# Constants as transposed rows, and roots and exponentials side by side, in a matmul-bound kernel

## The chip, the cores and the metric

One core of a Trainium2 chip. The metric is device time in microseconds (us) of one execution, taken over several runs. Engines are called as the profile calls them: PE is TensorE, DVE is VectorE, ACT is ScalarE, POOL is GpSimd, SP is SyncE. "L501" is a line of the kernel's source, so the same statement has another number in another version.

## The reference, cut to what matters

```
xn  = layernorm(x)                               # x: 2048 x 576, bf16
h_t = Lam_bar * h_{t-1} + B_bar xn_t             # 576 complex states, Lam_bar = exp(dt * Lambda), dt = exp(log_dt)
A   = 2 Re(C h) + xn * Dskip
B   = (sigmoid(xn Wg) * (xn Wu)) Wd              # 576 -> 4608 -> 576
out = x + A + B
```

Almost all the work is in B. The recurrence needs, per state, `exp` of `log_dt`, a decay, and tables of sines and cosines of angle times position. The constants are three vectors of 576 numbers: `log_dt`, `Lambda_re`, `Lambda_im`.

## The kernel before

The sequence is cut into four blocks of 512 rows. PE computes "groups": 18 matmuls of 64 x 128 by 64 x 512 that fill one pair of PSUM banks with gate and up values. ACT reads the pair (a sigmoid into `sT`, a copy into `uT`), and DVE multiplies them to `hT`. After 24 groups come eight down steps of 24 matmuls (later ones carry the matmuls of C as well; the last step has 42). Four PSUM pairs rotate (code cut and condensed here and below):

```
PE_SLOTS = 4
def ps_pair(name):
    return psum.tile([P, 2, TB], FP32, name=name, tag="ps")     # PE_SLOTS bufs
...
def evac(self):                                  # of a gate/up group
    nc.scalar.activation(sT[:], self.ps[:, 0, :], ACT.Sigmoid)
    nc.scalar.copy(uT[:], self.ps[:, 1, :])
    nc.vector.tensor_mul(h[:], sT[:], uT[:])
    bg.step(T_GROUP - 0.42 - 0.2)                # let DVE's background work go on
```

DVE's other work stands in a background queue that gets a credit of 1.33 us per group. At the start, block 0's LN goes through PE transposes. Then two groups start, and block 1's LN and the constants follow through the queue:

```
for g in start_groups: g.mms(slice(2 * P, TB))           # second halves of g0 and g1
for tt in range(4, 8): bg.add(1.05, lambda tt=tt: ln_stats(tt))
bg.gap()
bg.add(0.0, lambda: ln_std(1, 0, TT_B))                  # the square roots, on ACT
bg.add(0.2, lambda: ln_recip(1, 0, TT_B))
...                                                      # norms and DMA transposes of block 1
for tt in range(0, 8): bg.add(1.25, lambda tt=tt: ln_resid(tt))
bg.gap()
bg.add(1.0, exp_first, ready=lambda: consts_at[0] is not None and consts_at[0] + 4 <= bg.now)
bg.gap()
bg.add(1.5, angles_small)
...                                                      # ten angle tables of 1.35
bg.step(3.2)
for g in start_groups:
    g.evac(); used(g); bg.step(4.5)
```

The constants were fetched by nine loads on POOL's queue that scatter single numbers over partitions, 35 us into the profiled run (the end of the function is cut):

```
def load_consts():
    for (dst, src) in ((ldt, A_log_dt), (lre, A_Lambda_re), (lim, A_Lambda_im)):
        nc.gpsimd.dma_start(dst[:, 0:PT], src[0:R0].rearrange("(a p) -> p a", p=P))
        for h0 in (0, H):
            nc.gpsimd.dma_start(dst[h0:h0 + H, PT:NU], src[R0:NS].rearrange("(a b) -> a b", b=1))
```

## Time and profile before

| | before |
|---|---|
| time at the outset, median of 3 | 509.22 us (508.66 to 509.3) |
| the profiled run | 508.32 us, span 506.5 |
| PE, DVE, ACT, POOL busy | 99%, 64%, 40%, 19% |
| first real group starts | 8.48 |
| last matmul ends | 502.76 |

A timeline line has start, duration, engine, source line, operation, tiles and count; a bracket names idle time before it and what ended it. The waits view has total us, number of times and the longest. A view of one source line, used for the end of the program, has count, then duration in ns (least, median, most), then the first and the last start. The profiled run took 508.32 us and the timed runs 509.2.

### The profile page before, as it was taken

Reading aid. Unit: us, or ns where it says so; the run is one execution under the profiler, and the core shown is the slowest. Engines: PE = TensorE matmul, PEld = TensorE weight load, DVE = VectorE, ACT = ScalarE, POOL = GpSimd, SP = SyncE. Lnnn points to the kernel's source line nnn. Section 1 sums busy time; section 2 is a strip of 40 time slices with the busy share of each in tenths; the row PEclk is TensorE's granted clock in tenths of the full one; section 3 lists DMA queues with packets and bytes.
Section 4 is the critical chain, followed back from the end, with each engine's and each line's share of the span. In section 5 each row is a group of like instructions: output and inputs, shape, how many; then the busy total and the mean of one; then the engine's idle time right before and its main releaser. Section 6 shows DMA issues by size and latency. Waiting matters only on the chain.

```text
span 506.5 us, 10662 instructions
## 1 busy us (share of the span) xinstructions
PE 500.9 (99%) x4536; PEld 290.1 (57%) x4536; DVE 324.1 (64%) x703; ACT 204.9 (40%) x368; POOL 96.9 (19%) x143
## 2 busy tenths in 40 slices
PE   8999999999999999999999999999999999999997
PEld 6444575444477444477754444774444774446775
DVE  6964999886888797868878767786765222221111
ACT  4767623556500756520035655006555005553000
POOL 7138420123100043110001231000431001300000
PEclk9999999999999999999999999999999999999999
DMA  8999895246220099261430652200753201600001
GB/s 211 206 181 163 204 188 98 55 110 141 49 48 25 1 145 199 58 149 37 89 77 11 155 132 55 49 25 1 160 114 79 48 25 39 171 1 4 33 25 36
DMA packets 42959, 45.59 MB, mean 90 GB/s; under 512 B 30496, under 2 KB 34336, under 8 KB 42912
## 3 DMA queue, kind: packets, MB, share of 16 engines
q0 software_dynamic: 12672, 34.23, 31.1%
q1 hardware_dynamic: 29808, 10.33, 10.7%
q8 instruction: 35, 0.57, 0.5%
q10 hardware_dynamic: 432, 0.37, 0.2%
q14 instruction: 12, 0.10, 0.1%
HBM read 34.36 MB, written 2.36 MB: 72 GB/s over the span
## 4 chain that ended last, share of the span: by engine, by line
PE 94%; DVE 3%; ACT 1%; DMA 1%; issue 0%
PE pgu L495 52%; PE pd L569 34%; PE pbu L524 7%; DVE sctab L325 1%; DVE rnd L324 1%; DMA xt<-in_A_x_dram 1%; DVE ang L349 1%; PE ptr L741 0%; DVE hT L504 0%; ACT xT L744 0%; DVE bnst L224 0%; ACT L328 0%; ACT uT L502 0%; ACT L501 0%; ACT sT L501 0%
## 5 line engine op out<-in xcount | busy, mean ns | idle before, releaser
L495 PE MATMUL pgu<-xT,wgu 64*128 64x512 bf16 (+1 forms) x2628 | 283.7, 373 | 0.0
L495 PEld LDWEIGHTS <-wgu 64*128 64x128 bf16 x2628 | 127.6, 94 | 151.1 <-issue 0.5
L569 PE MATMUL pd<-wd,hT 128*128 128x288 bf16 x1152 | 144.8, 286 | 0.4 <-DVE hT L504 0.4
L501 ACT ACTIVATE sT<-pgu 128x512 bf16<-128x512 f32 x144 | 86.4, 600 | 120.4 <-PE pgu L495 110.3
L569 PEld LDWEIGHTS <-hT 128*128 128x128 bf16 x1152 | 112.1, 98 | 31.3 <-DVE hT L504 1.5
L504 DVE TENSOR_TENSOR hT<-sT,uT 128x512 bf16<-128x512 bf16 x144 | 60.7, 423 | 100.3 <-ACT uT L502 100.1
L502 ACT CAST uT<-pgu 128x512 bf16<-128x512 f32 x144 | 83.9, 583 | 0.0
L154 POOL DMA_DIRECT2D wgu<-in_B_w_gate_dram x36 | 27.9, 776 | 227.2 <-PE pgu L495 208.2
L160 POOL DMA_DIRECT2D wd<-in_B_w_down_dram x36 | 26.6, 755 | 100.2 <-PE pd L569 100.2
L530 ACT COPY bure<-pbu 128x512 f32<-128x512 f32 x16 | 9.4, 588 | 87.8 <-PE pbu L524 75.4
L589 DVE TENSOR_TENSOR acc<-acc,pd 128x576 f32<-128x576 f32 x32 | 24.1, 752 | 24.5 <-PE pd L569 24.5
L586 DVE TENSOR_TENSOR ob<-acc,pd 128x576 bf16<-128x576 f32 x15 | 11.3, 754 | 38.0 <-PE pd L569 38.0
L524 PE MATMUL pbu<-xT,bt 64*128 64x512 bf16 x288 | 33.7, 376 | 0.0
L569 PEld LDWEIGHTS <-hst 128*128 128x128 bf16 x288 | 28.2, 98 | 7.1
L154 POOL DMA_DIRECT2D wgu<-in_B_w_up_dram x36 | 26.8, 745 | 2.7 <-DMA wgu<-in_B_w_up_dram 1.9
L569 PE MATMUL pd<-ctre,hst 128*128 128x288 bf16 x128 | 26.5, 286 | 0.0
L569 PE MATMUL pd<-ctim,hst 128*128 128x288 bf16 x128 | 26.5, 286 | 0.0
L439 DVE TENSOR_TENSOR_SCAN gre<-r,g0re,wrim 128x512 bf16<-128x512 f32 x20 | 25.6, 1279 | 0.0
L524 PEld LDWEIGHTS <-bt 64*128 64x128 bf16 x288 | 13.7, 94 | 17.1 <-issue 0.7
L446 DVE TENSOR_TENSOR_SCAN gim<-r,g0im,wrim 128x512 bf16<-128x512 f32 x16 | 20.4, 1275 | 0.0
L224 DVE BATCH_NORM_STATS2 bnst<-xt 128x6 f32<-128x288 bf16 x32 | 12.6, 435 | 2.2 <-DMA xt<-in_A_x_dram 2.2
L501 ACT ACT_TABLE_LOAD x6 | 7.7, 1283 | 15.5 <-PE pgu L495 15.4
(113 smaller groups left out, 280.8 us busy)
## 6 DMA issues: line engine op xcount, KB each, us to landing
wgu<-in_B_w_gate_dram POOLq DMA_DIRECT2D x36, 288.0 KB, 4.4
wgu<-in_B_w_up_dram POOLq DMA_DIRECT2D x36, 288.0 KB, 5.2
wd<-in_B_w_down_dram POOLq DMA_DIRECT2D x36, 288.0 KB, 6.1
out_dram<-ob SPq DMA_DIRECT2D x15, 144.0 KB, 1.8
xt<-in_A_x_dram SPq DMA_DIRECT2D x10, 144.0 KB, 2.8
xt<-in_A_x_dram POOLq DMA_DIRECT2D x4, 144.0 KB, 6.6
bt<-ctre POOLq DMA_DIRECT2D x2, 288.0 KB, 7.2
bt<-ctim POOLq DMA_DIRECT2D x2, 288.0 KB, 8.0
```

Source lines behind the costliest of these rows:

```text
L154: eng.dma_start(w[rows, :, :], src[:, fs].rearrange("(c p) f -> p c f", p=H))
L160: nc.gpsimd.dma_start(wd[:], B_w_down[f0:f0 + FP * P, :].rearrange("(n p) d -> p n d", p=P))
L224: nc.vector.bn_stats(st[:, gi, :], xt[:, gi * DH:(gi + 1) * DH])
L439: nc.vector.tensor_tensor_scan(gre[:], r_bc, w[:, 0, :], g0re[:, col], ALU.mult, ALU.add)
L446: nc.vector.tensor_tensor_scan(gim[:], r_bc, w[:, 1, :], g0im[:, col], ALU.mult, ALU.add)
L495: nc.tensor.matmul(self.ps[:, gi, cols], w[rows, c, fs], xT[self.nb][rows, c, cols], start=c == 0, stop=c == NH - 1)
L501: nc.scalar.activation(sT[:], self.ps[:, 0, :], ACT.Sigmoid)
L502: nc.scalar.copy(uT[:], self.ps[:, 1, :])
L504: nc.vector.tensor_mul(h[:], sT[:], uT[:])
L524: nc.tensor.matmul(out, w, xT[self.nb][rows, c, ts_], start=c == 0, stop=c == NH - 1)
L569: nc.tensor.matmul(out, lhsT, rhs[:, a * DH:(a + 1) * DH], start=i == 0, stop=i == n - 1)
L589: nc.vector.tensor_add(halves(acc[:]), halves(acc[:]), pd[:, :, 0:DH])
```

## The change

The intent was to take the nine scattered loads off POOL's queue, to have the exponentials early so that the angle tables don't crowd the first down steps, to save one table load on ACT by putting roots and exponentials side by side, and to shorten the tail of the last step. The core of the diff, cut:

```
+    crows = consts.tile([3 * NH, H], BF16, name="crows")
+    for i, src in enumerate((A_log_dt, A_Lambda_re, A_Lambda_im)):
+        nc.sync.dma_start(crows[i * NH:(i + 1) * NH, :], src.rearrange("(a p) -> a p", p=H))
+    def consts_transpose(ps):
+        for half in (slice(0, H), slice(H, P)):
+            nc.tensor.transpose(ps[half, 0:3 * NH], crows[:], ident[0:3 * NH, 0:3 * NH])
+    def consts_copy(ps): ...                     # three copies on DVE, PSUM -> cvals
...
     def exp_first():
-        nc.scalar.activation(dt[:], ldt[:], ACT.Exp)
-        nc.vector.tensor_mul(r5[:], dt[:], lre[:])
-        nc.scalar.activation(r5[:], r5[:], ACT.Exp)
+        nc.scalar.activation(dt[:], ldt, ACT.Exp)
+        for a in range(NU):
+            nc.scalar.activation(r5[:, a:a + 1], lre[:, a:a + 1], ACT.Exp, scale=dt[:, a:a + 1])
...
-            for a, eng in ((0, nc.sync), (1, nc.scalar)):      # last step: 288 + 288 columns
+            for eng, cs in ((nc.sync, slice(0, D - P)), (nc.scalar, slice(D - P, D))):   # 448 + 128
...
-    for g in start_groups:
-        g.mms(slice(2 * P, TB))
-    ...                                          # the queue shown above
+    start_groups[0].mms(slice(2 * P, TB))
+    consts_transpose(ptrs[1][:, NH, :])
+    consts_copy(ptrs[1][:, NH, :])
+    start_groups[1].mms(slice(2 * P, TB))
+    for tt in range(TT_B, 2 * TT_B): ln_stats(tt)
+    for g in start_groups: g.evac(); used(g)
+    ln_std(1, 0, TT_B)
+    exp_first()
+    ln_recip(1, 0, TT_B)
+    ...                                          # norms and transposes in place, then the residuals and angles in the queue
```

More of the change, by code (lines that the diff above doesn't have):

```diff
@@ L166 @@
         load_x(tt, nc.sync if tt % 2 == 0 else nc.scalar)
-    for pr in range(2):
-        load_wgu((0, pr), nc.gpsimd, nc.gpsimd)
+    load_wgu((0, 0), nc.gpsimd, nc.gpsimd)
+    load_wgu((0, 1), nc.gpsimd, nc.gpsimd)
     for tt in range(TT_B, 2 * TT_B):
@@ L184, with consts_copy @@
     xn_bufs = [consts.tile([P, NH, 2, H], BF16, name=f"xn{i}") for i in range(XN_BUFS)]
-    lre = consts.tile([P, NU], FP32, name="lre")
-    lim = consts.tile([P, NU], FP32, name="lim")
-    ldt = consts.tile([P, NU], FP32, name="ldt")
-    consts_at = [None]
-    def load_consts():
-        for (dst, src) in ((ldt, A_log_dt), (lre, A_Lambda_re), (lim, A_Lambda_im)):
-            nc.gpsimd.dma_start(dst[:, 0:PT], src[0:R0].rearrange("(a p) -> p a", p=P))
-            for h0 in (0, H):
-                nc.gpsimd.dma_start(dst[h0:h0 + H, PT:NU], src[R0:NS].rearrange("(a b) -> a b", b=1))
-        consts_at[0] = bg.now
+    cvals = consts.tile([P, 3, NU], FP32, name="cvals")
+    ldt, lre, lim = (cvals[:, i, :] for i in range(3))
+    crows = consts.tile([3 * NH, H], BF16, name="crows")
[4 more added lines that the diff above has]
+            nc.tensor.transpose(ps[half, 0:3 * NH], crows[:], ident[0:3 * NH, 0:3 * NH])
+    def consts_copy(ps):
+        rows = ps[:, 0:3 * NH].rearrange("p (i a) -> p i a", a=NH)
+        nc.vector.tensor_copy(cvals[0:H, :, :], rows[0:H, :, 0:NH:2])
+        nc.vector.tensor_copy(cvals[H:P, :, 0:PT], rows[H:P, :, 1:NH:2])
+        nc.vector.tensor_copy(cvals[H:P, :, PT:NU], rows[H:P, :, NH - 1:NH])
     iota = ssmp.tile([P, TB], FP32, name="iota", tag="buim", bufs=2)
@@ L327, in exp_first @@
     def exp_first():
-        nc.scalar.activation(dt[:], ldt[:], ACT.Exp)
-        nc.vector.tensor_mul(r5[:], dt[:], lre[:])
-        nc.scalar.activation(r5[:], r5[:], ACT.Exp)
+        nc.scalar.activation(dt[:], ldt, ACT.Exp)
+        for a in range(NU):
+            nc.scalar.activation(r5[:, a:a + 1], lre[:, a:a + 1], ACT.Exp, scale=dt[:, a:a + 1])
     def angles_small():
-        nc.vector.tensor_mul(thc[:], dt[:], lim[:])
+        nc.vector.tensor_mul(thc[:], dt[:], lim)
         nc.vector.tensor_scalar_mul(thc[:], thc[:], 1.0 / TWO_PI)
@@ L365, in per_state_q @@
         nc.vector.tensor_mul(ni[:], r5[:], sn)
-        nc.vector.tensor_mul(m1[:], lre[:], lre[:])
-        nc.vector.tensor_mul(m2[:], lim[:], lim[:])
+        nc.vector.tensor_mul(m1[:], lre, lre)
+        nc.vector.tensor_mul(m2[:], lim, lim)
         nc.vector.tensor_add(m1[:], m1[:], m2[:])
         nc.vector.reciprocal(m1[:], m1[:])
-        nc.vector.tensor_mul(qre[:], nr[:], lre[:])
-        nc.vector.tensor_mul(m2[:], ni[:], lim[:])
+        nc.vector.tensor_mul(qre[:], nr[:], lre)
+        nc.vector.tensor_mul(m2[:], ni[:], lim)
         nc.vector.tensor_add(qre[:], qre[:], m2[:])
         nc.vector.tensor_mul(qre[:], qre[:], m1[:])
-        nc.vector.tensor_mul(qim[:], ni[:], lre[:])
-        nc.vector.tensor_mul(m2[:], nr[:], lim[:])
+        nc.vector.tensor_mul(qim[:], ni[:], lre)
+        nc.vector.tensor_mul(m2[:], nr[:], lim)
         nc.vector.tensor_sub(qim[:], qim[:], m2[:])
@@ L572, in d_step @@
             ob = lnp.tile([P, D], BF16, name="ob", bufs=2)
-            for a, eng in ((0, nc.sync), (1, nc.scalar)):
-                cs = slice(a * DH, (a + 1) * DH)
-                pd = ps_pair("pd")
+            for eng, cs in ((nc.sync, slice(0, D - P)), (nc.scalar, slice(D - P, D))):
+                pd = ps_pair("pd")[:, 0, 0:cs.stop - cs.start]
                 for i in range(n):
-                    mm(pd[:, 0, 0:DH], i, a)
-                nc.vector.tensor_add(ob[:, cs], acc[:, cs], pd[:, 0, 0:DH])
+                    lhsT, rhs = terms[i]
+                    nc.tensor.matmul(pd, lhsT, rhs[:, cs], start=i == 0, stop=i == n - 1)
+                nc.vector.tensor_add(ob[:, cs], acc[:, cs], pd)
                 eng.dma_start(o[tt * P:(tt + 1) * P, cs], ob[:, cs])
@@ L726 @@
     start_groups = [GateUp(0, f, 0) for f in range(2)]
-    ptrs = [psum.tile([P, NH, P], BF16, name="ptr", tag="ps") for _ in range(2)]
+    ptrs = [psum.tile([P, NH + 1, P], BF16, name="ptr", tag="ps") for _ in range(2)]
     for g in start_groups:
@@ L770 @@
         start_copy(tt, slice(5, NH), nc.vector.tensor_copy)
-    for g in start_groups:
-        g.mms(slice(2 * P, TB))
-    for tt in range(TT_B, 2 * TT_B):
-        bg.add(1.05, lambda tt=tt: ln_stats(tt))
-    bg.gap()
-    bg.add(0.0, lambda: ln_std(1, 0, TT_B))
-    bg.add(0.2, lambda: ln_recip(1, 0, TT_B))
-    for tt in range(TT_B, 2 * TT_B):
-        bg.add(0.9, lambda tt=tt: ln_norm(tt))
-        bg.add(0.0, lambda tt=tt: ln_dma_transpose(tt))
-    bg.add(0.0, lambda: ln_done.add(1))
-    bg.add(0.0, bg.owe)
+    start_groups[0].mms(slice(2 * P, TB))
+    consts_transpose(ptrs[1][:, NH, :])
+    consts_copy(ptrs[1][:, NH, :])
+    start_groups[1].mms(slice(2 * P, TB))
+    for tt in range(TT_B, 2 * TT_B):
+        ln_stats(tt)
+    for g in start_groups:
+        g.evac()
+        used(g)
+    ln_std(1, 0, TT_B)
+    exp_first()
+    ln_recip(1, 0, TT_B)
+    for tt in range(TT_B, 2 * TT_B):
+        ln_norm(tt)
+        ln_dma_transpose(tt)
+    ln_done.add(1)
+    bg.owe()
     for tt in range(0, 2 * TT_B):
         bg.add(1.25, lambda tt=tt: ln_resid(tt))
-    bg.gap()
-    bg.add(1.0, exp_first, ready=lambda: consts_at[0] is not None and consts_at[0] + 4 <= bg.now)
-    bg.gap()
     bg.add(1.5, angles_small)
@@ L791 @@
             bg.add(1.35, lambda pt=pt, which=which: angle(pt, which))
-    bg.step(3.2)
-    for g in start_groups:
-        g.evac()
-        used(g)
-        bg.step(4.5)
     def catch_up_ln(nb):
@@ L821 @@
                 run_groups([GateUp(slot, f, nb) for (f, nb) in order[:8]])
-                catch_up_ln(1)
                 order = order[8:]
-                side_loads.extend([load_consts] + bt_loads)
+                side_loads.extend(bt_loads)
             run_groups([GateUp(slot, f, nb) for (f, nb) in order])
```

## The prediction

> **What bounds the kernel now.** I read the page's busy times first, then who TensorE waited for, then the engines' timelines in the first 64 us and the last 12 us.
>
> ```profile
> PE 500.9 (99%) x4536; PEld 290.1 (57%) x4536; DVE 324.1 (64%) x703; ACT 204.9 (40%) x368; POOL 96.9 (19%) x143
> ...
> PE pgu L733 <- DVE warm L182: 1.3, 1, 1.3
> PE pd L569 <- DVE hT L504: 0.4, 1, 0.4
> PE ptr L741 <- DVE xn L249: 0.3, 1, 0.3
> ```
>
> TensorE is busy 500.9 of 506.5 us. Its recorded waits sum to 2.0 us, and only one of them lies in the body: 0.4 us before the first down-projection matmuls, behind an hT. Busy alone proves little for a pipelined engine, so I check the pitch: in the chain of waits a gate/up group (18 matmuls of 512 columns) takes 1.94 us, 108 ns each, and the last down step advances every 0.122 us per 288 columns. The work is thus 144 groups x 1.94 = 279.8, the state inputs 4 x (4 x 1.94 + 0.98) = 35.0, and the down and C matmuls 1440 x 0.1224 = 176.3: together 491.1 us. Between the first real group at 8.48 and the last matmul at 502.76 lie 494.3 us, 1.1 of which are input transposes. The body holds barely 2 us that a schedule could win. Any change of this kind is worth tenths, unless it makes TensorE stop.
>
> What it could win or lose is in the start, on ACT and DVE:
>
> ```profile
> 11.61 1.28 ACT L501 ACT_TABLE_LOAD   x1
> 12.90 0.60 ACT L501 ACTIVATE sT<-pgu 128x512 bf16<-128x512 f32 x1
> 13.39 0.58 ACT L502 CAST uT<-pgu 128x512 bf16<-128x512 f32 x1
> 13.99 1.28 ACT L228 ACT_TABLE_LOAD   x1
> 16.16 0.30 ACT L228 ACTIVATE rstd<-mv,eps_t 128x4 f32<-128x4 f32 x1 [0.89 <-DVE mv L225]
> 16.48 1.28 ACT L501 ACT_TABLE_LOAD   x1
> 17.77 0.60 ACT L501 ACTIVATE sT<-pgu 128x512 bf16<-128x512 f32 x1
> 18.26 0.58 ACT L502 CAST uT<-pgu 128x512 bf16<-128x512 f32 x1
> 18.73 0.61 ACT L501 ACTIVATE sT<-pgu 128x512 bf16<-128x512 f32 x1
> ```
>
> This is ACT's timeline. The first sigmoid group (I count groups g0, g1, ... in emission order) is evacuated at 12.90, then ACT loads the square-root table, waits 0.89 us for the last statistics, takes the roots, and loads the sigmoid table again. g1 is read only at 17.77. From a later undisturbed group (g11, read at 33.28, as it ends) and 1.943 us per group, g1 ended at 33.28 - 10 x 1.943 = 13.85. It was read 3.9 us late and TensorE did not feel it, because four PSUM pairs rotate.
>
> ```profile
> 42.14 1.28 ACT L328 ACT_TABLE_LOAD   x1
> 43.44 0.21 ACT L328 ACTIVATE dt<-ldt 128x5 f32<-128x5 f32 x1
> 43.88 0.21 ACT L330 ACTIVATE r<-r 128x5 f32<-128x5 f32 x1 [0.23 <-DVE r L329]
> 44.10 1.28 ACT L501 ACT_TABLE_LOAD   x1
> 45.40 0.60 ACT L501 ACTIVATE sT<-pgu 128x512 bf16<-128x512 f32 x1
> ...
> 59.23 0.42 DVE L504 TENSOR_TENSOR hT<-sT,uT 128x512 bf16<-128x512 bf16 x1
> ...
> 59.70 2.50 PE L569 MATMUL pd<-wd,hT 128*128 128x288 bf16 x19 [0.35 <-DVE hT L504]
> ```
>
> ACT, then DVE, then TensorE. The exponentials come 30 us later with two more table loads. The angle tables wait for them, so DVE starts the angles only at 48.2 with credit saved up. From there each hT stands behind one angle until 59.65, when the last hT of the first down step appears. TensorE lost 0.35 us to it.
>
> **What the Trainium skill says.** "ScalarE: Activation LUTs", section "What ACT_TABLE_LOAD costs", has about 1283 ns for the load plus about 1380 ns of drain per switch. The trace agrees on the load (1.28 us at all four places above) but shows no drain: a load starts 0.01 us after the copy's end (13.39 + 0.58, next at 13.99) and the activation follows it 0.01 us later. I count 1.28. Section "Table sets: the hidden batching unit" says to batch by set; roots and exponentials are in different sets there, so putting them side by side saves one return to sigmoid, not a load of its own. The trace's 12 loads should become 11. "Perfetto Trace Analysis", section "Matmuls", says that independent groups should rotate through PSUM banks so that evacuation overlaps matmuls; this kernel rotates four pairs, which is the limit that I use below. "TensorE: Matmul & The Clock Gate", section "Back-to-back issue gap", has about 81 ns per matmul of 128 columns with its weight load; here 20 warm-up matmuls of that size, each with its weight load, start from 7.14 to 8.2 us, 56 ns apart, and I use that.
>
> **The change part by part.**
> (a) Constants. Nine descriptor-poor loads on the POOL queue (35.0 to 40.5 us, 5.5 us of POOL) become three row loads on SP behind the first x tiles. TensorE never waited for a weight load in that stretch, so 0 on the path. In their place stand two tiny transposes between g0's and g1's second halves (0.1 us of TensorE) and three small copies on DVE. I put a copy at 0.2 us, from the 0.17 us of the other 5-column DVE operations plus a little for PSUM: 0.6 us.
> (b) LN of block 1 in place. The DVE copies of xT ended at 12.04, and the statistics began at once. Now DVE must wait for the transposes, which follow the end of g0, 13.85 - 0.97 = 12.88, plus some 0.25 for their latency: 13.15. Copies until 13.75. Four statistics at 0.94 (three took 11.96 to 14.78): 17.5. Before, they ended at 16.13, with one hT between them, which now comes after.
> (c) ACT. g0 and g1 are now read by 15.1 with no switch between, and the root table is loaded while ACT waits. Roots 17.5 to 17.8 (0.30). Exp table to 19.1. dt 0.21: 19.3. Then five exponentials of one column, each with a pointer scale; the two one-column roots at 8.31 took 0.49 together, so a pitch of 0.2 and 1.1 us for the five: 20.4. Sigmoid table to 21.7. sT of g2 21.7, its uT from 22.2 to 22.75 (pitch 0.49, length 0.58).
> (d) The PSUM rotation. g6 takes the pair of g2. Unhindered, g6 would start when g5 ends: 13.95 + 4 x 1.943 = 21.72, with the 0.1 of (a). It can't start before 22.75 or so. In general the reading of g2 may be late by 3 x 1.943 - 1.07 = 4.76 us; before the change the lateness at this place was 3.9 (g1), now it is 21.7 - 15.9 = 5.8. So TensorE stops for about 1.0 us, once. g7 needs g3, read by 23.7, and starts at 24.7: the backlog melts, as ACT needs 0.95 us a group against 1.94. This is on the path that sets the end, since TensorE has no slack to give it back: +1.0.
> (e) xT of block 1. The first norm ends at about 18.8 instead of 17.5, so the four DMA transposes shift by 1.25 us. The last was issued at 23.62 with a median landing of 4.6, so 28.2; now about 29.5. The first group of block 1, g10, starts at 29.4 + 1.1 = 30.5. Just hidden: 0.
> (f) The background. Eight residual steps of 1.25, then 1.5, then ten angles of 1.35: 25.0 of credit (the kernel's own budget in us), against -2 + 22 x 1.33 = 27.3 for the 22 groups left (the kernel grants 1.95 - 0.42 - 0.2 a group). Walking the credit through, the first angle falls at g13 and the last at g22. An angle and an hT take 1.58 + 0.34 = 1.92 us of DVE per 1.94 us group, so DVE keeps level, and the hT of g21 is ready 2 us or more ahead of its use. The 0.35 us wait goes: -0.35.
> (g) The last step, split 448 + 128 instead of 288 + 288. 21 matmuls x 0.190 (0.1224 x 448/288) = 4.0, and 21 x 0.056 = 1.2, against 2 x 2.57 = 5.14: +0.05. The last add falls from 0.46 to about 0.30 (0.75 at 576 columns and 0.46 at 288 give 1.0 ns a column): -0.16. The last store is 32 KB instead of 72, where 72 took 1.6 us and 144 took 1.8: -0.1. The first store starts about 0.5 us before TensorE ends, so it lands first. Sum -0.2.
>
> Sum: +0.1 + 1.0 - 0.35 - 0.2 = +0.55, on 509.22: 509.8. The 1.0 is the weakest term, a difference of two nearly equal times.
>
> **Rivals.** One: no stop. If the exponentials or the copies are quicker than I took them by 1 us in all, g2 is read in time, and only the gains of (f) and perhaps (g) stay: 508.8 to 509.0. For it: the lateness of 3.9 us was absorbed before; against it: three table loads of 1.28 now stand between g1 and g2 where two stood between g0 and g1, though one of them is hidden in a wait. Two: the stop is longer, or comes twice. If constants land late or a drain of the kind that the skill names appears at the back-to-back loads, 1.4 us more on ACT give 511.2; block 1's xT would then still be no bound, as g10 moves too. For it stands the skill's figure alone; against it the exponentials at 43.88, 0.21 us long, after which the next load starts at 44.10 with no drain. Three: xT of block 1 is the bound. DMA transposes took up to 12.7 us to land elsewhere, and constants, weights and x share the engines early on (DMA share 1.0 around 20 to 40 us). A landing 2 us later than my estimate would cost about 1 us in place of the stop at g6 or on top of it: 510.8 to 511.
>
> **Range and chances.** The three rivals span 508.8 to 511.2; runs of the same kernel spread 0.6 us. I take 509.8 with 508.7 to 511.1 for 8 in 10. A change of 2% is 10.2 us, more than all of these together, in either direction: 0.01 faster, 0.98 same, 0.01 slower.
>
> **What would show it.** TensorE's waits should lose the entry on hT at the first down step and gain one of about 1 us on ACT's uT near 22 us. ACT's timeline should show the roots at 17.5, the reading of g2 at 21.7, and 11 table loads in all. The last angle should end before 56 us. The last 128-column part should take about 1.2 us and end at the same distance from the span's end as before, within 0.3. If TensorE shows no wait near 22 us, step (d) is wrong and the kernel is some 0.4 us faster than before; if g10 waits for a DMA near 30 us, (e) is.

## The result, and the profile after

The changed kernel takes 508.43 us (median of 6, 508.30 to 508.74) against 509.25 (median of 6, 508.66 to 509.30) in the same rounds. The ratio is 0.9987 with a 95% interval of 0.9974 to 1.0000. Ratios here are the mean time of one kernel's fast runs over that of the other's in the same rounds, so they are not quite the ratio of the medians. By the 2% measure this is "same", as the forecast's chances had it. But the forecast said 0.6 us slower with a range from 508.7, and the measured median lies below it.

The busy line of the changed kernel's page, and the wait of its PE after the warm-up:

```profile
PE 501.5 (99%) x4538; PEld 292.5 (58%) x4538; DVE 324.7 (64%) x705; ACT 204.4 (40%) x371; POOL 90.8 (18%) x134
```

```profile
PE pgu L501 <- ACT uT L508: 0.8, 1, 0.8
```

PE is as busy as before. The wait on `hT` at the first down step is gone, and a stop of 0.8 us on `uT` has come. ACT's timeline of the changed kernel, from the root table's load on (g1's reading ended at 15.39):

```profile
15.41 1.28 ACT L234 ACT_TABLE_LOAD   x1
17.57 0.30 ACT L234 ACTIVATE rstd<-mv,eps_t 128x4 f32<-128x4 f32 x1 [0.87 <-DVE mv L231]
17.88 1.28 ACT L334 ACT_TABLE_LOAD   x1
19.18 0.21 ACT L334 ACTIVATE dt<-cvals 128x5 f32<-128x5 f32 x1
19.42 1.03 ACT L336 ACTIVATE r<-cvals,dt 128x1 f32<-128x1 f32 x5
20.46 1.28 ACT L507 ACT_TABLE_LOAD   x1
21.75 0.60 ACT L507 ACTIVATE sT<-pgu 128x512 bf16<-128x512 f32 x1
22.25 0.58 ACT L508 CAST uT<-pgu 128x512 bf16<-128x512 f32 x1
```

Roots at 17.57, exponentials from 19.18 to 20.45, g2 read from 21.75 to 22.83: within 0.1 us of steps (b) and (c). The root's bracket says what it waited for: 0.87 us for the statistics of DVE, which had itself waited for the transposes of the constants (behind g0's second half on PE). DVE's and then PE's timeline:

```profile
13.23 0.17 DVE L201 CAST cvals<-ptr 64x15 f32<-64x15 bf16 x1 [0.96 <-PE ptr L196]
```

```profile
12.99 0.20 PE L196 MATMUL ptr<-ident,crows 27*64 27x27 bf16 x2
13.12 8.93 PE L501 MATMUL pgu<-xT,wgu 64*128 64x256 bf16 x90
22.88 35.14 PE L501 MATMUL pgu<-xT,wgu 64*128 64x512 bf16 x324 [0.83 <-ACT uT L508]
57.95 12.30 PE L575 MATMUL pd<-wd,hT 128*128 128x288 bf16 x99
```

PE stands still until 22.88, when the pair that g2 filled has been read; the view counts 0.83 us of idle time. After that it runs to the end; the down step at 57.95 has no bracket.

The idle time of this view is less than what PE loses. It runs from the modelled end of the last matmul, 0.38 us after that matmul's start, while inside a group the next start follows after 0.21. In the trace g6's first matmul starts 1.21 us after g5's last: a loss of 1.0 us. In the same way the 0.35 us before the first down step of the kernel before was a step of 0.64 where 0.12 is usual, a loss of 0.52.

So the trace shows the forecast stop nearly to the tenth, and yet the kernel is not slower. To find the rest I cut each profiled span into three: the start, up to the first matmul of a real group; the body, from there to the end of the last matmul; and the end. Each is read from PE's timeline and the span.

| profiled run | start | body | end | span |
|---|---|---|---|---|
| before | 8.48 | 494.28 | 3.76 | 506.5 |
| after | 8.70 | 495.00 | 2.95 | 506.7 |

The body grew by 0.72, near the forecast's +0.8 (0.1 + 1.0 - 0.35 + 0.05), but the end shrank by 0.81, not by 0.2. And these two profiles together say +0.1 us, while the timed runs say -0.8: the profiled run of before can't be a typical one.

### The profile page after: what moved, and what is told of

The parts are those of the page before. It is cut to its first block, busy times and chain, and to the rows that moved or that the text cites. A ratio compares the mean times of both kernels' runs of the same rounds, so it can differ in the third digit from the quotient of the medians.

```text
span 506.7 us, 10667 instructions
## 1 busy us (share of the span) xinstructions
PE 501.5 (99%) x4538; PEld 292.5 (58%) x4538; DVE 324.7 (64%) x705; ACT 204.4 (40%) x371; POOL 90.8 (18%) x134
## 4 chain that ended last, share of the span: by engine, by line
PE 97%; ACT 1%; DVE 1%; issue 0%
PE pgu L501 54%; PE pd L575 34%; PE pbu L530 7%; PE pd L583 1%; PE pgu L739 1%; DVE bnst L230 1%; PE ptr L747 0%; ACT xT L750 0%; ACT L507 0%; ACT L334 0%; ACT r L336 0%; DVE mv L231 0%; ACT uT L508 0%; ACT rstd L234 0%; DVE ob L584 0%
## 5 line engine op out<-in xcount | busy, mean ns | idle before, releaser
L501 PEld LDWEIGHTS <-wgu 64*128 64x128 bf16 x2628 | 130.2, 94 | 149.4 <-issue 1.6
L575 PE MATMUL pd<-wd,hT 128*128 128x288 bf16 x1128 | 141.3, 286 | 0.0
L575 PEld LDWEIGHTS <-hT 128*128 128x128 bf16 x1128 | 109.9, 98 | 30.1 <-issue 0.8
L575 PEld LDWEIGHTS <-hst 128*128 128x128 bf16 x270 | 26.4, 98 | 6.7
L575 PE MATMUL pd<-ctre,hst 128*128 128x288 bf16 x120 | 24.5, 286 | 0.0
L575 PE MATMUL pd<-ctim,hst 128*128 128x288 bf16 x120 | 24.5, 286 | 0.0
L432 DVE TENSOR_TENSOR tq<-T,buim 128x512 bf16<-128x512 bf16 x20 | 13.7, 685 | 0.0
```

The source lines that it names most:

```text
L501: nc.tensor.matmul(self.ps[:, gi, cols], w[rows, c, fs], xT[self.nb][rows, c, cols], start=c == 0, stop=c == NH - 1)
L575: nc.tensor.matmul(out, lhsT, rhs[:, a * DH:(a + 1) * DH], start=i == 0, stop=i == n - 1)
```

## The experiments

All were run with five rounds. Each call had its own chip and its own runs of the kernel before, whose median was 509.37 (first), 509.10 (second) and 509.41 (third); all runs were correct. In the table the body is cut once more: up to the first matmul of the first down step, and that step, up to the next gate/up matmul. What follows takes 422.12 us in all fourteen profiles. The times are read from each trace's PE records:

| kernel | time, median | ratio to before (95%) | start | body | to the first down step | that step | end |
|---|---|---|---|---|---|---|---|
| before | 509.25 | 1 | 8.48 | 494.28 | 48.01 | 24.15 | 3.76 |
| before_again | 509.10 | 0.9995 (0.9982 to 1.0007) | 9.15 | 494.72 | 48.01 | 24.60 | 3.71 |
| tail_only | 509.49 | 1.0006 (0.9993 to 1.0020) | 8.64 | 494.89 | 48.64 | 24.13 | 3.85 |
| before_shift3 | 508.89 | 0.9992 (0.9979 to 1.0004) | 9.06 | 494.72 | 48.01 | 24.60 | 3.51 |
| before_rows | 508.85 | 0.9994 (0.9981 to 1.0006) | 8.87 | 494.60 | 48.24 | 24.24 | 3.22 |
| after | 508.43 | 0.9987 (0.9974 to 1.0000) | 8.70 | 495.00 | 49.25 | 23.63 | 2.95 |
| after_again | 508.48 | 0.9988 (0.9974 to 1.0001) | 8.57 | 495.03 | 49.28 | 23.63 | 2.94 |
| after_oldtail | 508.78 | 0.9986 (0.9974 to 0.9998) | 8.67 | 495.00 | 49.25 | 23.63 | 3.21 |
| after_dose | 509.54 | 1.0000 (0.9986 to 1.0014) | 8.98 | 495.96 | 50.22 | 23.62 | 2.95 |
| copies_late | 507.81 | 0.9967 (0.9955 to 0.9979) | 8.41 | 494.32 | 48.57 | 23.63 | 2.93 |
| copies_mid | 507.84 | 0.9974 (0.9962 to 0.9987) | 9.14 | 494.13 | 48.39 | 23.63 | 2.93 |
| mid_pool9 | 507.74 | 0.9966 (0.9953 to 0.9979) | 8.58 | 494.13 | 48.38 | 23.63 | 3.22 |
| mid_shift | 507.53 | 0.9961 (0.9948 to 0.9974) | 8.53 | 494.21 | 48.46 | 23.63 | 2.74 |
| mid_shift_oldtail | 508.13 | 0.9971 (0.9958 to 0.9985) | 9.24 | 494.13 | 48.39 | 23.63 | 3.03 |

Three things are seen at a glance. Where PE isn't disturbed by a transfer or by DVE's backlog, the body repeats to 0.03 us, once 0.08 (495.00, 495.03, 495.00 for the changed kernel, 494.13 three times and 494.21 once for copies_mid and its kin), and the end goes by kinds of program. The first down step takes 23.63 us wherever PE doesn't wait in it, and 0.50 to 0.97 more in the five kernels of the old kind.

The start, on the other hand, wanders between 8.41 and 9.24 with no regard to the program. It goes with PE's warm-up, ten matmuls of 512 columns and six of 128. They start 0.43 and 0.11 us apart at first, and 0.22 and 0.056 from some moment on, which lies between about 4.2 us (after_again) and 7.3 us (mid_shift_oldtail). In six profiles it comes so late that the transposes behind the warm-up still begin at the slow step; these are the six latest starts, 8.87 to 9.24. The other eight start at 8.41 to 8.70. The Trainium skill ("TensorE: Matmul & The Clock Gate", section "What's actually happening") says that the clock's activity window is free-running and that the moment of the transition varies from run to run. The moments agree with that, but they lie 3 us apart, where the section has ±0.5 us; no run here shows the window itself. Two single times can thus differ by 0.8 us for this reason alone, and the parts of the span tell more.

### before_again: is the profiled run typical?

Edit: none.

> The kernel before, unchanged, to learn whether its one profiled run (508.32 us, span 506.5) stands for its timed runs (median 509.25). Theory A: it does not; most runs carry some 0.9 us in the program that the profiled one happened to miss, so the spans listed here scatter between 506.5 and 507.5 with a median near 507.4. Theory B: the time outside the span differs and the spans stay near 506.5. Ratio to the kernel before 1.000 in either case. If the profile is again one of the long runs, it shows where the 0.9 us lies.

Measured: spans from 507.1 to 507.9 in its five runs, none as short as 506.5. Theory A holds. The profile fell on a longer run, and shows at the first down step (PE's waits, POOL's timeline):

```profile
PE pd L569 <- DMA wd<-in_B_w_down_dram: 0.4, 1, 0.4
PE pd L569 <- DVE hT L504: 0.2, 1, 0.2
```

```profile
50.35 0.71 POOL L160 DMA_DIRECT2D wd<-in_B_w_down_dram  x1 [0.77 <-DMA wgu<-in_B_w_up_dram]
```

Here the last down weights were missing as well as an `hT`. POOL issued the last of those six loads at 50.35, after it had waited for an earlier load of its own queue to land (the bracket); in the profiled run of before, all six had been issued by 47.83. The nine scattered loads stand ahead of them in the same queue, from 35.7 to 42.6 us in this run. That they made the weights late is argued from this order and not shown: the three other profiles with the nine loads have no wait for down weights. But the prediction's sentence "TensorE never waited for a weight load in that stretch" doesn't hold for every run.

### tail_only: the last split alone

```
-            for a, eng in ((0, nc.sync), (1, nc.scalar)): ...
+            for eng, cs in ((nc.sync, slice(0, D - P)), (nc.scalar, slice(D - P, D))): ...
```

> The kernel before with only the last down step split 448 + 128. In the two profiles the time from the last matmul to the end was 3.74 us before and 3.0 after, where the prediction had 0.2 us in all for this part. Theory A: the new split is worth about 0.7 us by itself (508.5 from 509.2), all of it between the issue of the last store and the end. Theory B (the prediction): 0.2 us (509.05).

Measured: nothing (509.49), so theory A falls: the 0.7 us of the changed kernel's shorter end don't come from the split alone. Theory B's 0.2 is within the scatter (the interval is -0.4 to +1.0 us). The end was 3.85 us long; the last store took 1.9 us from issue to landing here, where the others of its size took 1.5 (from the issue to the first wait of SP after it). Why it did in this run is open. The body's 494.89 contains a wait of 0.3 us on `hT` (0.50 lost) and half a microsecond in which a pair of gate/up weights landed late, at 18.3 us.

### after_oldtail: the changed kernel without the new split

```
-            for eng, cs in ((nc.sync, slice(0, D - P)), (nc.scalar, slice(D - P, D))): ...
+            for a, eng in ((0, nc.sync), (1, nc.scalar)): ...
```

> The changed kernel with the old last split of 288 + 288: only the start differs from the kernel before. By the trace of the change the start loses 0.83 (stop on uT of the third group) + 0.15 (transposes) and wins 0.35. Theory A (the tail carries the gain): 0.6 us slower than the kernel before if its timed runs are like its profiled one, 509.8. Theory B (the kernel before loses some 0.9 us at the start in most runs, which the change removes): about 509.1, equal to before or a little faster.

Measured: 508.78, 0.9986 of before. It is faster than before although its body is as long as that of the changed kernel, 495.00. That is near theory B. Its end is 3.21: only 0.26 us longer than with the new split, and half a microsecond shorter than before's, with the same last step. So something outside the last step shortened the end.

### before_shift3 and before_rows: what shortened the end?

The trace has an answer to try. At the end, the sequencer of SP goes through the completion semaphores of all transfers in a fixed order, one wait after the other. SP's and ACT's transfers take eight semaphores in turn, as the trace's records have them. For before and then for after, two fences each: the last add and store in the timeline; then, among the instructions that close the program, SP's waits from the last landing on and POOL's drain and clear:

```profile
502.79 0.46 DVE L578 TENSOR_TENSOR ob<-acc,pd 128x288 bf16<-128x288 f32 x1 [2.12 <-PE pd L569]
503.28 0.35 ACTq L579 DMA_DIRECT2D out_dram<-ob  x1
```

```profile
L884 SPq EVENT_SEMAPHORE  x9: 17/28/28, 504.9 to 506.5; - x9
L884 POOLq DRAIN  x2: 46/74/102, 505.6 to 506.2; - x2
L884 POOLq EVENT_SEMAPHORE_RANGE_CLEAR  x1: 139/139/139, 506.1 to 506.1; - x1
```

```profile
503.73 0.29 DVE L584 TENSOR_TENSOR ob<-acc,pd 128x128 bf16<-128x128 f32 x1 [0.55 <-PE pd L583]
504.06 0.36 ACTq L585 DMA_DIRECT2D out_dram<-ob  x1
```

```profile
L887 SPq EVENT_SEMAPHORE  x6: 17/28/28, 505.6 to 506.6; - x6
L887 POOLq DRAIN  x2: 40/71/102, 506.1 to 506.4; - x2
L887 POOLq EVENT_SEMAPHORE_RANGE_CLEAR  x1: 139/139/139, 506.2 to 506.2; - x1
```

Two of SP's waits in each fence belong to a barrier. So from the wait that the last landing ends, that one included, there are seven before the change and four after, 0.06 us apart. The last store had the second of the eight semaphores, and has the fifth: the three small loads of rows moved every later transfer three places on. There is a second difference: POOL's clear of the semaphores starts, in the trace's finer times, 0.34 us after its drain ends (505.73 to 506.07) before, and 0.03 us after it (506.18 to 506.21) in the changed kernel.

```
+    crows = consts.tile([3 * NH, H], BF16, name="crows")        # before_shift3: loaded, never used
+    for i, src in enumerate((A_log_dt, A_Lambda_re, A_Lambda_im)):
+        nc.sync.dma_start(crows[i * NH:(i + 1) * NH, :], src.rearrange("(a p) -> a p", p=H))
```

> The kernel before plus three tiny loads of the constants' rows on SP whose data nobody uses. They do nothing but move every later SP and ACT transfer three places on in the rotation of eight completion semaphores, so that the last store signals the fifth of them, as in the changed kernel, and not the second. Theory A: the time from the issue of the last store to the end falls from 3.2 to about 2.7 us, because the sequencer of SP goes through the semaphores in order after the last landing; timed 0.5 us faster than before. Theory B: the shorter end of the changed kernel has another cause; the end stays at 3.2 us and the time is that of before within 0.2.

Measured: the end is 3.51, 0.20 to 0.25 below before's 3.71 and 3.76, and four waits are left:

```profile
L888 SPq EVENT_SEMAPHORE  x6: 17/28/28, 505.9 to 507.2; - x6
```

```profile
PE pd L573 <- DVE hT L508: 0.8, 1, 0.8
```

The semaphores' order is real, but worth 0.2 and not 0.5; the gap at POOL stayed (0.32). The time fell by 0.2 in the median, which the scatter nearly hides. The profile of this run also shows the longest `hT` wait of all, 0.8 us, and nothing in its edit was meant to touch it: in the five profiles of the old kind the first down step loses 0.50, 0.52, 0.61, 0.97 and 0.97 us.

```
# before_rows, cut: load_consts gone; rows, consts_transpose after g0's second half, consts_copy behind the first statistics
-    for g in start_groups: g.mms(slice(2 * P, TB))
+    start_groups[0].mms(slice(2 * P, TB)); consts_transpose(ptrs[1][:, NH, :]); start_groups[1].mms(slice(2 * P, TB))
```

> The kernel before with one part of the change: the constants come as rows through TensorE, and the nine loads on the POOL queue are gone. Roots, exponentials and the last split stay where they were. It has the three SP loads, so it also has what before_shift3 has. Theory A (the POOL loads delay the down weights and in some runs hold TensorE at the first down step): beyond before_shift3 it wins a further 0.2 to 0.5 us on average less 0.15 for the transposes, and its runs scatter less (0.5 us instead of 1.8). The wait on hT of 0.35 us stays. Theory B: as before_shift3 plus 0.15, with the same scatter.

Measured: 508.85, no better than before_shift3, with runs from 508.45 to 509.16. Neither theory says what happened. The end fell to 3.22, by 0.29, and the gap at POOL is 0.03: so it goes with the nine loads. The body gained 0.12 against the profile of before_shift3, although the transposes make PE reach the first down step 0.23 later (48.24 for 48.01). But a wait on `hT` stays:

```profile
PE pd L579 <- DVE hT L514: 0.4, 1, 0.4
```

So taking the loads away doesn't cure the first down step. In all nine profiles with the early exponentials that wait is gone, as the prediction had it; no run moves the exponentials alone. Whether the loads had delayed the down weights can't be told from this, as before_shift3's profile has no such wait either.

### mid_pool9: is it the number of POOL's transfers?

```
+    def pool_loads():                            # three whole rows each, never used
+        for i in range(9):
+            nc.gpsimd.dma_start(scrap[i * 3:(i + 1) * 3, :], A_log_dt[0:3 * H].rearrange("(a p) -> a p", p=H))
-                side_loads.extend(bt_loads)
+                side_loads.extend([pool_loads] + bt_loads)
```

(on top of copies_mid, told below.)

> Copies_mid with nine loads of three whole rows each on the POOL queue, at the place where the kernel before had its nine loads of the constants, but with few large pieces. In the traces POOL's last semaphore clear came 0.32 to 0.34 us after its drain in the kernels with nine more POOL loads, and 0.03 us after it in those without. If the number of POOL's instructions makes this, the gap is back here and the time is 0.3 above copies_mid, 508.1, with no wait at the first down step. If it was the many small pieces of the constants' loads, the gap stays at 0.03 and the time at 507.85.

Measured: the gap is back. POOL's drain and clear in mid_pool9:

```profile
L894 POOLq DRAIN  x2: 46/70/93, 505.1 to 505.7; - x2
L894 POOLq EVENT_SEMAPHORE_RANGE_CLEAR  x1: 139/139/139, 505.5 to 505.5; - x1
```

The drain ends at 505.16, the clear starts at 505.48, and the end is 3.22 against 2.93 in copies_mid. The first down step has no wait and the body is 494.13. So nine more transfers in POOL's program cost 0.29 us at the end of the profiled run, whether they scatter single numbers or bring whole rows. The expected 508.1 was missed (507.74), and the timed runs don't show the 0.29: copies_mid ran on another chip, and its profiled run started at 9.14, this one at 8.58. Against mid_shift in the same rounds (507.53) mid_pool9 is 0.21 slower, where the ends differ by 0.48. Why POOL's sequencer is late there isn't shown.

### after_dose: is the stop on the path, one for one?

```
-        for a in range(NU):
+        for a in 2 * list(range(NU)):            # the five exponentials twice, the same values
```

> The changed kernel with the five one-column exponentials done twice over the same values: 1.03 us more on ACT between the roots and the third group's reading (the five took 1.03). If every microsecond of ACT there lies on TensorE's path once g2 is read too late, the stop grows from 0.83 to about 1.9 us and the time by 1.0, to 509.5. Rival: the stop is hidden or made up later; then the time grows by less than 0.4.

```profile
PE pgu L501 <- ACT uT L508: 1.8, 1, 1.8
```

Measured: the idle time grew from 0.83 to 1.76 us, the body by 0.96, and the time to 509.54, no faster than before. The ten exponentials took 1.96 us where five took 1.03: for 0.93 us of ACT, 0.96 us of body. Step (d) holds: past its tolerance, time between the roots and g2's reading lies on the path, one for one.

### copies_late and copies_mid: can the stop be taken away?

The roots waited 0.87 us for statistics that had waited for the constants. If the copies of the constants don't stand ahead of the statistics, both waits should vanish, and 0.87 is most of the 1.0 us that PE lost.

```
     consts_transpose(ptrs[1][:, NH, :])
-    consts_copy(ptrs[1][:, NH, :])
     start_groups[1].mms(slice(2 * P, TB))
     for tt in range(TT_B, 2 * TT_B):
         ln_stats(tt)
+        if tt == TT_B: consts_copy(ptrs[1][:, NH, :])          # copies_mid
+    consts_copy(ptrs[1][:, NH, :])                             # copies_late, instead
```

> The changed kernel with the three copies of the constants moved behind the statistics of block 1 on DVE, so that the statistics need not wait for the transposes. If the stop of 0.83 us before g6 comes from the roots being at 17.57 (of which ACT waited 0.87 for the statistics), the roots come at about 16.7, g2 is read at about 20.9 and the stop vanishes: 0.7 to 0.9 us faster than the changed kernel, about 507.6. Rival: the constants or something else then hold the exponentials and the stop stays: 508.4.

> The changed kernel with the three copies behind the first of block 1's four statistics. DVE has then no wait for the transposes, and the PSUM pair of the constants is free by 13.8, so the wait of 0.15 us on the copies that copies_late showed before its fourth group should go, and the roots come at about 16.8. Expected 507.7, 0.1 to 0.2 faster than copies_late and 0.8 faster than the changed kernel. If the stop stays above 0.3 us, the statistics were not what held the roots.

Measured: 507.81 and 507.84; after_again, in the same rounds as copies_mid, had 508.48. ACT in copies_mid, whose start was 0.44 us later than that of the profiled changed kernel:

```profile
15.85 1.28 ACT L234 ACT_TABLE_LOAD   x1
17.14 0.30 ACT L234 ACTIVATE rstd<-mv,eps_t 128x4 f32<-128x4 f32 x1
21.32 0.60 ACT L507 ACTIVATE sT<-pgu 128x512 bf16<-128x512 f32 x1
```

PE's waits in copies_late:

```profile
PE pgu L501 <- DVE cvals L203: 0.2, 1, 0.2
```

The root follows its table load with no wait. g2 is read 12.18 us after the first group's start (21.32 - 9.14) and not 13.05 (21.75 - 8.70), and PE's waits view is empty after the warm-up. The start of g6 shows that the stop isn't quite gone: its first matmul starts 0.34 us after g5's last and not 0.21. Against before_rows, which has the transposes and no stop, copies_mid comes to the first down step 0.15 later (48.39 for 48.24). In copies_late PE waited 0.15 us (0.2 in the view, 0.33 lost) for a copy, because g3 needs the PSUM pair that holds the constants. In copies_mid this is gone. The bodies are 494.32 and 494.13 against 495.00. The medians of the two don't differ; they come from different chips, and the start wanders by more than 0.19.

> The changed kernel unchanged, for a comparison in the same rounds with the others: 508.4 if it repeats. Copies_mid should stand 0.7 to 0.9 us below it.

Measured: 508.48, 0.64 above copies_mid, a little under the expected 0.7 to 0.9; the bodies differ by 0.90. The changed kernel itself repeats within 0.05.

### mid_shift and mid_shift_oldtail: the best version

```
+    crows2 = ...                                 # three more unused row loads on SP, on top of copies_mid
```

> Copies_mid with three more tiny unused row loads on SP, so that the last store signals the eighth and last completion semaphore. In the trace of the change four semaphore waits of 0.06 us follow the last landing; here one should be left, 0.19 us less. Expected 507.65, 0.2 below copies_mid (507.84). Rival: the order does not matter or the loads disturb the start: 507.8 or more.

Measured: 507.53, and an end of 2.74, the expected 0.19 less. From the last landing on SP has one wait left (three less two of the barrier):

```profile
L892 SPq EVENT_SEMAPHORE  x3: 17/17/27, 504.6 to 505.4; - x3
```

It is the fastest of all, 0.9961 of before.

> The same with the old last split of 288 + 288. After_oldtail stood 0.3 us above the changed kernel, though on another chip, and tail_only showed nothing. If the split is worth its 0.17 us of a shorter add and 0.1 of a quicker landing, this is 0.25 us slower than mid_shift; if tail_only was right, the two are equal within 0.1.

Measured: 508.13 with an end of 3.03. The split is worth 0.29 at the end; the remaining 0.3 of the timed difference is not in body or end, and the profiled start was 0.7 us later. With after against after_oldtail (0.26), this is the second pair that gives the split about 0.27, and tail_only the one that doesn't.

## Why the prediction was wrong, step by step

- **The bound, and no change of 2%.** Right. Neither start nor body nor end moved by a whole microsecond.
- **(a) constants.** The transposes cost about 0.2 us of PE's chain and not 0.1 (before_rows reaches the first down step at 48.24 and not 48.01). "0 on the path" for the loads is in doubt: before_again waited for down weights that stood behind them.
- **(b), (c) the times on ACT.** Right to 0.1 us: roots 17.5 and 17.57, g2 read at 21.7 and 21.75, 11 table loads and no drain. The copies took 0.43 us and not 0.6.
- **(d) the stop at g6.** Right in place, cause, kind and size: 1.0 us forecast and 1.0 lost (49.25 less 48.24; the waits view has 0.83), shown on the path by after_dose and, for 0.87 of it, taken away by copies_mid.
- **(e) block 1's transposed x.** Right: no wait there.
- **(f) the wait on hT, -0.35: the second term that was mis-sized.** The wait went, as did the angles from the last groups' way: they start at 40.08, behind g13, and the last follows g22. (It ends at 60.0 and not before 56: g22 itself ends on PE only at about 56.0, a group's 1.94 us before the down step at 57.95. The `hT` of g21 was there in time all the same.) But 0.35 is what one bracket of one run showed. By the step of the matmuls that run lost 0.52, and the four profiles with the nine loads (before, before_again, tail_only, before_shift3) lost 0.52, 0.97, 0.50 and 0.97 at the first down step, on average 0.74, part of it in before_again to down weights. Tail_only lost 0.63 more ahead of it, most of it to late gate/up weights. I took the first for the rule. The page of one profile was no help here; its run of 508.32 against timed runs of 509.2 was the warning that I passed over.
- **(g) the last step, -0.2: the step that failed.** It was right as far as it went: the split left the body as it was and changed the end by about -0.27. But (g) took the last add and the last store for all that could change at the end, and the end of the program has other terms. Three loads more on SP moved the last store to a later semaphore (-0.2), and nine transfers fewer on POOL took away a gap ahead of its last clear (-0.29). The end fell by 0.8 in all.

Two small misreadings of the prediction cost nothing: its lines show five table loads and not four, and the load follows the copy by 0.02 us, not 0.01.

The sum as measured, from the means of the four old profiles: +1.0 for the stop, +0.2 for the transposes, -0.9 for what the old kind lost to waits up to the first down step's end (0.74, and a quarter of tail_only's 0.63), -0.8 at the end: -0.5 us, against -0.66 by the ratio (0.0013 of 509.25), whose interval runs from -1.3 to 0. Of the forecast's error, 0.6 lies in (g) and 0.5 in (f) and the late weights, less 0.1 in (a); the rest is within the scatter of the start. Rival one ("no stop") came closest to the time, 508.8 to 509.0, for a reason that the traces refute.

What stays open: why POOL's clear is late with nine more transfers, why tail_only's last store landed late, whether the nine loads delayed the down weights, and how often each of the waits at the first down step occurs, as only five profiles of the old kind exist.

## What to carry to other kernels

Where the bound engine is at 99%, read what the neighbours' lateness may be before it costs anything: here three groups' time less one reading, by the prediction's estimate 4.76 us. Up to it lateness was free (3.9 us before the change); past it each microsecond counted. Read what a stop costs from the step between matmuls, as the idle time of the view was 0.2 us short here. A small copy can be expensive through what stands behind it on its engine: three copies of 0.17 us, waiting 0.96 us in front of the statistics, cost 0.9 us of kernel and moving them by one place gave that back. And before differences from one profile are added to a median, compare that profile's own time with the median: a run that is 0.9 us quicker than the rest doesn't show what the rest suffers.

## What the Trainium skill lacked or had wrong

- "ScalarE: Activation LUTs", section "What ACT_TABLE_LOAD costs", adds a drain of about 1380 ns to each switch of sets. No switch in these traces shows one (the next activation starts within 0.06 us, or behind an idle time that ends with its input), not even with loads nearly back to back: an activation ends at 17.87, the load starts at 17.88 and takes 1.28, and the next activation starts at 19.18.
- "TensorE: Matmul & The Clock Gate", section "Back-to-back issue gap", has about 81 ns for sustained matmuls of 128 columns with their weight loads. Here 21 of them took 1.18 us (5.16 for both parts of the last step, less 21 x 0.1895 for the 448 columns), 56 ns each, which is the section's own figure for an isolated one.
- No page has what the end of a program costs by its own transfers: 0.06 us for each completion semaphore that SP goes through from the last landing on (one to seven of them here), and 0.3 us more ahead of POOL's last clear in programs with nine more POOL transfers. It would belong to "Runtime: NRT & Kernel Launch", beside the launch sequence.
